# Sums of blocks in place of block products in the second layer of a routed mixture of experts

## The chip, the cores and the metric

The kernel runs on one core of a Trainium2 chip. The core has a matrix engine (TensorE, PE in the profile), a vector engine (VectorE, DVE), a scalar engine (ScalarE, ACT), a general engine (GpSimd, POOL), a queue for transfers (SyncE, SP) and 16 DMA engines. The metric is the device time of one execution in microseconds (us), lower being better.

## The reference

The program is an RWKV-5 attention followed by a balanced mixture of experts, all in float32.

```python
for t in range(S):                        # attention: B=4, H=8, S=768, D=48
    cur = einsum('bhd,bhe->bhde', u*k[t], v[t])
    y[t] = einsum('bhd,bhde->bhe', r[t], state + cur)
    state = w*state + einsum('bhd,bhe->bhde', k[t], v[t])
x = y as 3072 tokens of 384
logits = x @ w_gate                       # 8 experts, 384 tokens each, given out greedily
for e in range(8):                        # w1[e]: 384 x 1024, w2[e]: 1024 x 384
    h = maximum(x[mask_e] @ w1[e], 0)
    out[mask_e] = h @ w2[e]
```

The change touches the last line: for each expert a product of a 384x1024 and a 1024x384 matrix.

## The kernel before, in words

The first 130 us or so are the attention (class `Mild`), in units of 128 time steps, with its order on the engines written out by hand. It leaves the tokens as rows in DRAM (`x_rows`) and the logits in `LG`.

Which tokens an expert gets is found on the chip (class `Assignment`). For each expert, `likely_steps` runs three rounds: VectorE compares the best logits with 16 thresholds (`ind`), TensorE counts (`counts`, L901), VectorE sums up (`own`, `cnt`, `wide`), TensorE spreads the sum over the partitions (L912), and VectorE narrows the thresholds (`most` to `cand`, `low`). Then come the expert's number (`fmax`), two small matmuls (`st_ps`) and the places of its tokens. `tokens` makes a list of token numbers from the places with the matmuls `some_ps` (L1365) and `list_ps` (L1383). `fetch` then gathers the token rows with GpSimd (`xg`, L1468) and loads the expert's weights over SP (L1461): w1 and then w2, 1.5 MB each. The weights and `xg` lie in two turns of buffers, so expert n's weights can be loaded when expert n-2 is done with them. Routing for expert n+1 is written ahead of expert n's layers.

The expert that gets enough tokens in the first part of the sequence is treated first with 256 tokens (`early`, lines L1539 and L1547), interleaved by hand with the routing of the next ones; its other 128 tokens come last. Between these, seven experts with all their 384 tokens are treated in `Experts.run`. For each:

- `turn` transposes the gathered rows (L1483), three blocks of 128 tokens.
- `hidden` (L1492) makes the hidden layer turned: 8 blocks j of 128 hidden numbers, each with three matmuls of 384 columns (all tokens), and a relu on ScalarE (L1494) into `hid`.
- `result` (L1504) makes the second layer for one block c of 128 tokens: 8 matmuls, over j, with `hid[:, j, block c]` as the stationary operand and `w2[:, j, :]` (384 columns) streamed. ScalarE copies the sum out (L1510) and GpSimd scatters the rows to the output (L1498). The transposes of the next expert stand ahead of the last block.

In this part a scheduler orders each engine's instructions when the program is built. It interleaves the routing with the matmuls; the order is fixed on the chip[...]. The call that names the next expert's routing is one line, at the head of each expert:

```python
ahead = next(later, None)
hid = self.hidden(w1, xT, nb * 128)
```

A second form of the whole computation stands behind a branch on `have["ok"]`, for inputs on which the quick routing doesn't hold.

Of the kernel before, what the change touches and what calls it, by code (L numbers as in the profile page):

```python
# [10 lines left out]
F32 = mybir.dt.float32  # L11
# [5 lines left out]
ALU = mybir.AluOpType  # L17
# [671 lines left out]
class Assignment:  # L689
# [716 lines left out]
def rwkv5_eagle_then_base_layer_balanced(  # L1406
# [12 lines left out]
    nc = tc.nc  # L1419
    N, DX = out.shape  # L1420
    E, _, F = moe_w1.shape
    NT = N // 128
# [13 lines left out]
    o_last = keep.tile([128, DX], F32, name="o_last")  # L1436
    tok_last = keep.tile([128, 1], I32, name="tok_last")

    class Experts:

        def __init__(self):
# [4 lines left out]

        def open_rest(self, ctx, **how):
            pool = lambda name, bufs, **kw: ctx.enter_context(tc.tile_pool(name=name, bufs=bufs, **kw))
            self.h, self.o = pool("f_h", 2, **how), pool("f_o", 3, **how)
            self.ps_t, self.ps_h, self.ps_o = (pool(f"f_ps_{x}", 2, space=PSUM) for x in "tho")  # L1450

        def load_weights(self, n, fmax):
            number = walk.outs.tile([1, 1], I32, name="number")
            nc.vector.tensor_scalar(out=number, in0=fmax[0:1, :], scalar1=1.0, scalar2=float(E),
                                    op0=ALU.max, op1=ALU.min)
            pool = self.turns[n % 2]
            w1, w2 = pool.tile([128, KD, F], F32, name="w1"), pool.tile([128, KF, DX], F32, name="w2")
            e = nc.values_load(number[0:1, 0:1], engines=(mybir.EngineType.SP,), min_val=1, max_val=E,
                               skip_runtime_bounds_check_because="held between 1 and E")
            for t, src in ((w1, moe_w1), (w2, moe_w2)):  # L1460
                nc.sync.dma_start(t, src[ds(E - e, 1)].rearrange("o (c p) f -> p (o c) f", p=128))  # L1461
            return w1, w2

# [20 lines left out]
                nc.scalar.copy(xT[:, :, ts(c, 128)], xT_ps)  # L1484
            return xT

        def hidden(self, w1, xT, m):
            hid = self.h.tile([128, KF, CAP], F32, name="hid")
            for j in range(KF):
                h_ps = self.ps_h.tile([128, CAP], F32, name="h_ps")  # L1490
                for f in range(KD):
                    nc.tensor.matmul(h_ps[:, 0:m], w1[:, f, ts(j, 128)], xT[:, f, 0:m],  # L1492
                                     start=(f == 0), stop=(f == KD - 1))
                nc.scalar.activation(hid[:, j, 0:m], h_ps[:, 0:m], AF.Relu)  # L1494
            return hid

        def scatter(self, o_sb, tok, to):
            nc.gpsimd.indirect_dma_start(out=to, out_offset=bass.IndirectOffsetOnAxis(ap=tok, axis=0),  # L1498
# [14 lines left out]
        def run(self, ahead, later, rows):  # L1513
            xT = self.turn(ahead)
            while ahead:
                _, _, tok, w1, w2 = ahead
                nb = tok.shape[1]
                ahead = next(later, None)
                hid = self.hidden(w1, xT, nb * 128)
                for c in range(nb):  # L1520
                    if c == nb - 1 and ahead:
                        xT = self.turn(ahead)
                    self.result(c, hid, w2, tok, next(rows))
# [31 lines left out]
    with ExitStack() as whole:  # L1555
        x = Experts()
        for i in range(2):
            x.open(whole, i)
        rows = iter(out_rows)
        have = {}  # L1560
        first = walk.new_outs()
        with ExitStack() as part:
            mild = Mild(tc, r, k, v, w, u, moe_w_gate, x_dram, LG, ident, walk)
            mild.open(part)
            epool = part.enter_context(tc.tile_pool(name="f_early", bufs=1))

# [12 lines left out]
            def step(n, at):  # L1579
                for _ in range(steps.count((n, at))):  # L1580
                    next(early)

            with tc.manual_schedule():
                two, one = mild.run(step)
                NE = walk.EARLY // 128
                pieces = x.early(mild.ps, epool, *have["w"], *have["x"], rows, have)

                def go(m):
                    for _ in range(m):
                        next(pieces, None)  # L1590
# [12 lines left out]
                tok = walk.tokens(first["place"])  # L1603
                walk.between = lambda: None
                xg = x.gather(1, tok)
                to = walk.in_order(tok)
                walk.leave(first)
                next(early)
                have["to"] = walk.in_order(have["x"][1])
                second = walk.new_outs()  # L1610
                search = walk.likely_steps(**second)
                go(6)
                for m in (2, 3, 2, 3):
                    next(search)
                    go(m)
                go(99)
                walk.book(first, first=True)
        x.open_rest(whole, reuse_waits="tile")

        def later():  # L1620
            for _ in search:
                pass
            walk.bound(ident)
            was = second
            walk.book(was)
            walk.leave(was)
            for n in range(2, E):
                rest = n == E - 1
                now = walk.remainder() if rest else walk.event()
                walk.book(now, surely=rest)  # L1630
                walk.choose(was, now)
                yield x.fetch(n, was["fmax"], walk.tokens(was["place"]))
                if not rest:
                    walk.leave(now)
                was = now
            tc.mark_branch_hint_location("whole")
            have["ok"] = walk.found()
            yield x.fetch(E, walk.star, walk.tokens(walk.star_place, 1))

        x.run((1, xg, to, *have["v"]), later(), (a for a in [*out_rows[2:NT - 1], None]))  # L1640

    with tc.If(have["ok"] < 1, label="whole", preferred_fallthrough_block=False):
        with ExitStack() as arm:
            attention_any(arm, tc, r, k, v, w, u, moe_w_gate, x_dram, LG, ident, walk)
        walk.restart()
        with ExitStack() as arm:
            x = Experts()
            for i in range(2):
                x.open(arm, i)
            x.open_rest(arm)  # L1650
            x.run(x.fetch(0, *walk.general_fill()),
                  (x.fetch(n, *walk.general_fill()) if n < E - 1 else x.fetch(n, *walk.last_fill())
                   for n in range(1, E)), iter([out] * (NT - 1) + [None]))
    x.scatter(o_last, tok_last, out_rows[NT - 1])


# [26 lines left out]
```

## Time and profile before

| | |
|---|---|
| median of 3 runs | 416.0 us (415.75 to 416.31) |
| the profiled execution's own time | 415.83 us |
| its span, first to last instruction | 414.1 us, mean granted TensorE clock 0.989 |
| busy: PE, weight loads (PEld), DVE, ACT, POOL | 394.4, 268.3, 200.0, 153.6, 134.6 us |
| hidden layer L1492, all records | 122.2 us |
| second layer L1504, all records | 117.6 us |
| weights of an expert | 2 transfers of 1536 KB |

A line of the timeline has the start (us from the span's start), the duration, the engine, the line of the program, the operation, the tiles written and read, shapes, and how many instructions are merged; in brackets, how long the engine was idle before it and what ended that. Float32 matmuls have two records each. A table by stretches gives each engine's busy time and the number of its instructions in each stretch of the span, the granted clock (PEclk), the share of the DMA engines and their rate.

### The profile page before, as it was taken

To read this page: it belongs to the slowest core of one execution; us is meant where nothing else is said; L and a number is where in the kernel's file an instruction comes from. 1 tells how busy PE (TensorE), PEld (TensorE's weight loads), DVE (VectorE), ACT (ScalarE), POOL (GpSimd) and SP (SyncE) were. 2 spreads that over 40 slices of the span, in tenths; PEclk is the share of its full clock that TensorE was granted. 3 is DMA by queue.
4 is the path that set the end of the run, shared out by engine and by line. 5 is a ranking of instruction groups with operands and counts; after the bars stand their busy time and mean duration, and the time that the engine had idled before them with its cause. 6 is when DMAs were issued, how large, how long until landed. Compare 5 with 4: busy or idle time off the path is not lost.

```text
span 414.1 us, 7993 instructions
## 1 busy us (share of the span) xinstructions
PE 394.4 (95%) x2981; PEld 268.3 (65%) x2981; DVE 200.0 (48%) x794; ACT 153.6 (37%) x401; POOL 134.6 (33%) x172
## 2 busy tenths in 40 slices
PE   5999999999999888999999999999999999999993
PEld 4778888888877655555556555555655655655581
DVE  5776776576885788780580381273074050010000
ACT  2597888788872312212121120221221221212120
POOL 5597878566732022004104103103002121110100
PEclk9799999999999999999999999999999999999998
DMA  9999998887591282047045137109108653350010
GB/s 123 163 154 195 197 169 153 157 169 156 123 321 41 78 298 101 2 142 258 21 180 201 38 91 291 39 10 352 38 21 311 240 173 109 138 190 5 19 39 25
DMA packets 95298, 57.25 MB, mean 138 GB/s; under 512 B 77201, under 2 KB 89490, under 8 KB 95250
## 3 DMA queue, kind: packets, MB, share of 16 engines
q1 hardware_dynamic: 91520, 47.19, 45.7%
q0 software_dynamic: 3072, 9.44, 6.4%
q8 instruction: 25, 0.41, 0.4%
q14 instruction: 23, 0.19, 0.2%
q10 hardware_dynamic: 658, 0.01, 0.1%
HBM read 47.20 MB, written 9.44 MB: 137 GB/s over the span
## 4 chain that ended last, share of the span: by engine, by line
PE 71%; DMA 12%; DVE 6%; issue 5%; ACT 2%; POOL 1%; POOLq 0%; ACTq 0%; DVEq 0%
PE h_ps L1492 21%; PE o_ps L1504 19%; DMA out_dram<-o_sb,to 11%; PE y_ps L532 7%; PE g_ps L494 5%; PE kT_ps L456 3%; PE kv_ps L511 3%; PE rT_ps L462 2%; PE x_ps L581 2%; PE e_o_ps L1547 2%; PE lg_ps L561 2%; PE xT_ps L1483 2%; ACT AT L484 1%; PE e_h_ps L1539 1%; POOL xg L1468 1%
## 5 line engine op out<-in xcount | busy, mean ns | idle before, releaser
L1492 PE MATMUL h_ps<-xT,w 128*128 128x384 f32 (+1 forms) x384 | 122.2, 469 | 0.6 <-ACT xT L1484 0.6
L1504 PE MATMUL o_ps<-w,hid 128*128 128x384 f32 x352 | 117.6, 487 | 0.0
L1504 PEld LDWEIGHTS o_ps<-w,hid 128*128 128x128 f32 x352 | 65.4, 190 | 42.4 <-issue 0.8
L1492 PEld LDWEIGHTS h_ps<-xT,w 128*128 128x128 f32 x384 | 65.6, 190 | 36.5 <-issue 3.6
L1494 ACT ACTIVATE hid<-h_ps 128x384 f32<-128x384 f32 (+1 forms) x64 | 29.7, 464 | 92.2 <-PE h_ps L1492 85.3
L484 ACT ACTIVATE AT<-ident,dd 128x128 f32<-128x128 f32 x192 | 58.7, 390 | 2.1 <-DVE dd L443 1.9
L1468 POOL DMA_INDIRECT xg<-x_rows,tok x22 | 21.3, 966 | 116.2 <-issue 58.9
L1498 POOL DMA_INDIRECT out_dram<-o_sb,to x21 | 20.8, 993 | 98.1 <-ACT o_sb L1510 66.4
L1510 ACT COPY o_sb<-o_ps 128x384 f32<-128x384 f32 x21 | 10.1, 479 | 95.5 <-PE o_ps L1504 86.8
L498 DVE COPY_PREDICATED AT<-mask,g_ps 128x512 f32<-128x512 uint8 x48 | 32.6, 734 | 12.5 <-PE g_ps L494 12.2
L889 DVE TENSOR_TENSOR own<-counts,same 128x64 f32<-128x64 f32 x21 | 4.7, 225 | 65.5 <-PE counts L901 65.5
L494 PE MATMUL g_ps<-rT,kT 48*128 48x128 f32 x384 | 28.2, 287 | 0.6 <-DVE AT L498 0.6
L431 POOL TENSOR_TENSOR kss<-krs,wk 128x384 f32<-128x384 f32 x24 | 24.3, 1015 | 10.7 <-DVE krs L340 9.0
L494 PEld LDWEIGHTS g_ps<-rT,kT 48*128 48x128 f32 x384 | 23.6, 189 | 3.8 <-PE rT_ps L462 0.8
L532 PE MATMUL y_ps<-AT,vts 128*64 128x128 f32 x384 | 25.7, 276 | 0.0
L438 POOL TENSOR_TENSOR rk<-rk,u_bc 128x384 f32<-128x384 f32 x24 | 24.2, 1008 | 3.7 <-ACT u_bc L407 1.9
L437 POOL TENSOR_TENSOR rk<-krs 128x384 f32<-128x384 f32 x24 | 24.5, 1019 | 0.0
L532 PEld LDWEIGHTS y_ps<-AT,vts 128*64 128x64 f32 x384 | 20.6, 137 | 1.0 <-issue 0.5
L550 ACT COPY x<-y_ps 128x512 f32<-128x512 f32 x24 | 14.0, 585 | 15.9 <-PE y_ps L532 15.9
L474 DVE TENSOR_TENSOR rT<-rT_ps,WR 112x512 f32<-112x512 f32 x23 | 15.8, 685 | 4.4 <-PE rT_ps L462 4.3
L462 PE MATMUL rT_ps<-ident,krs 128*112 128x128 f32 x96 | 15.3, 285 | 0.0
L581 PE MATMUL x_ps<-ident,x 112*128 112x112 f32 x96 | 13.3, 262 | 1.4 <-ACT xr L588 0.7
(270 smaller groups left out, 464.6 us busy)
## 6 DMA issues: line engine op xcount, KB each, us to landing
w<-in_moe_w_dram SPq DMA_DIRECT2D x18, 1536.0 KB, 8.3
krs<-in_k_dram SPq DMA_DIRECT2D x24, 192.0 KB, 4.1
krs<-in_r_dram SPq DMA_DIRECT2D x24, 192.0 KB, 4.7
vts<-in_v_dram SPq DMA_DIRECT2D x24, 192.0 KB, 4.5
x_rows<-xr SPq DMA_DIRECT2D x24, 192.0 KB, 2.9
xg<-x_rows,tok POOLq DMA_INDIRECT x22, 4.7
out_dram<-o_sb,to POOLq DMA_INDIRECT x21, 2.6
wp<-in_w_dram SPq DMA_DIRECT2D x2, 0.4 KB, 2.0
```

The lines of the kernel that those rows point to most:

```text
L431: self.nc.gpsimd.tensor_mul(self.kss[:, n % self.NS].rearrange("p (g h) d -> p g h d", g=2)[:, :, :, 0:D], src, self.wk.rearrange("p (g h) ...
L437: nc.gpsimd.tensor_mul(rk, self.krs[:, n % self.NK, 1, 0:H, 0:D], self.krs[:, n % self.NK, 0, 0:H, 0:D])
L438: nc.gpsimd.tensor_mul(rk, rk, self.u_bc)
L462: nc.tensor.transpose(rT_ps[0:P, a, :], self.pair(kr[:, 1], a), self.ident)
L484: nc.scalar.mul(AT[:, z, a, :], self.ident, dd[:, h:h + 1])
L494: nc.tensor.matmul(g_ps[:, z, a, :], kT[rows, a, :], rT[rows, a, :], start=True, stop=True)
L498: nc.vector.copy_predicated(out=AT[:, z], mask=self.mask.unsqueeze(1).to_broadcast([128, HP, T]), data=g_ps[:, z])
L532: nc.tensor.matmul(yv[q * PD:(q + 1) * PD, o // 2, o % 2, :], lhsT, rhs, start=(o // 2, q) not in seen, stop=stop, skip_group_check=True)
L1468: nc.gpsimd.indirect_dma_start(out=xg[:, c, :], out_offset=None, in_=x_dram[0:within, :], in_offset=bass.IndirectOffsetOnAxis(ap=tok[:, c: ...
L1492: nc.tensor.matmul(h_ps[:, 0:m], w1[:, f, ts(j, 128)], xT[:, f, 0:m], start=(f == 0), stop=(f == KD - 1))
L1494: nc.scalar.activation(hid[:, j, 0:m], h_ps[:, 0:m], AF.Relu)
L1504: nc.tensor.matmul(o_ps, hid[:, j, ts(c, 128)], w2[:, j, :], start=(j == 0), stop=(j == KF - 1))
```

## The change

The second layer of the seven full experts is computed with fewer, smaller products and with sums of blocks.

In five experts (the first five in order) the first two blocks of tokens, the two halves of the hidden numbers and the two halves of the output columns form a product of two 2x2 matrices of blocks. It is made by seven products instead of eight. `S1` to `S4` are sums of hidden blocks, `T1` to `T4` sums of w2 blocks, and the outputs are sums of the products p1 to p7. Each product is four matmuls of 192 columns. The third block of tokens stays with `result`.

In the last two full experts (`many`) all three blocks, two halves and three column blocks of 128 form a 3x2 by 2x3 product, made by fifteen products instead of eighteen, each four matmuls of 128 columns. There are 10 sums of w2 blocks (`W...`), 11 of hidden blocks (`H...`) and 20 for the outputs.

All sums are instructions on VectorE. ScalarE copies the products out of PSUM in groups. Buffers for sums exist once each (`f_sums`, bufs=1), so a sum for the next expert is written when the product that reads the old one is done. w2 is loaded ahead of w1. Routing for the next expert is no longer all at the head of an expert: `later` yields between its steps, and `at_product` takes two steps during the products, so that the first count for the expert after the next stands in the second layer.

```diff
-            self.h, self.o = pool("f_h", 2, **how), pool("f_o", 3, **how)
+            self.h, self.o, self.sums = pool("f_h", 2, **how), pool("f_o", 2, **how), pool("f_sums", 1, **how)
...
-            for t, src in ((w1, moe_w1), (w2, moe_w2)):
+            for t, src in ((w2, moe_w2), (w1, moe_w1)):
...
                 nc.scalar.activation(hid[:, j, 0:m], h_ps[:, 0:m], AF.Relu)
+                if j == KF // 2 - 1:
+                    half(hid)
...
+        SEVEN_EARLY = (("S3", "h0", SUB, "h2"),)
+        SEVEN_LATE = (("S1", "h2", ADD, "h3"), ("S2", "S1", SUB, "h0"), ("S4", "h1", SUB, "S2"))
+        SEVEN = ((("p1", "h0", "w0"), ("p2", "h1", "w2")), (("p7", "S3", "T3"), ("p5", "S1", "T1")),
+                 (("p6", "S2", "T2"), ("p3", "S4", "w3")), (("p4", "h3", "T4"),))
...
+        EARLY_SUMS = (("H1", "h0", ADD, "h2"), ("H11", "h0", SUB, "h4"))
+        HID_SUMS = (("H8", "h1", ADD, "h3"), ("H7", "h1", SUB, "h0"), ("H9", "h1", SUB, "H11"),
+                    ("H3", "h5", SUB, "H9"), ("H0", "h1", ADD, "h2"), ("H6", "h3", ADD, "h5"),
+                    ("H5", "H11", ADD, "H6"), ("H2", "h2", SUB, "H6"), ("H12", "H2", ADD, "h4"))
...
+        PRODUCTS = ((("p4", "h4", "w1"), ("p1", "H1", "w2"), ("p11", "H11", "W11"), ("p10", "h5", "w4")),
+                    (("p8", "H8", "w5"), ("p13", "h1", "W13"), ("p7", "H7", "W7"), ("p9", "H9", "W9")),
+                    (("p3", "H3", "w3"), ("p0", "H0", "W0"), ("p14", "h2", "W14"), ("p5", "H5", "W5")),
+                    (("p12", "H12", "W12"), ("p6", "H6", "W6"), ("p2", "H2", "W2")))
...
+        def seven_w2(self, w2):
+            H, D = KF // 2, DX // 2
+            at = {f"w{2 * j + k}": w2[:, ts(j, H), ts(k, D)] for j in range(2) for k in range(2)}
+            self.sums_of(at, (("T3", "w3", SUB, "w1"), ("T1", "w1", SUB, "w0"), ("T2", "w3", SUB, "T1"),
+                              ("T4", "T2", SUB, "w2")), D)
+            return at
+
+        def sums_of(self, at, which, n=128):
+            for name, a, op, b in which:
+                kind = f"sum_{name[0] in 'TW'}_{sum(k[0] in 'TWSH' for k in at)}"
+                t = self.sums.tile([128, KF // 2, n], F32, name=name, tag=kind)
+                nc.vector.tensor_tensor(out=t, in0=at[a], in1=at[b], op=op)
+                at[name] = t
...
+        def products(self, products, out_sums, left, right, tok, rows, at_product, nk, ni):
...
+            for group, after in zip(products, out_sums):
+                m = len(group)
+                ps = self.ps_o.tile([128, m, D], F32, name="p_ps", tag="o_ps")
+                for q, (name, a, b) in enumerate(group):
+                    for j in range(KF // 2):
+                        nc.tensor.matmul(ps[:, q, :], left[a][:, j, :], right[b][:, j, :],
+                                         start=(j == 0), stop=(j == KF // 2 - 1))
+                    at[name] = res[:, n + q, :]
+                    at_product((n + q + 1) / count)
+                nc.scalar.copy(res[:, n:n + m, :], ps)
+                n += m
+                for name, a, op, b in after:
+                    if name not in at:
+                        at[name] = res[:, count + sum(k[0] not in "po" for k in at), :]
+                    nc.vector.tensor_tensor(out=at[name], in0=at[a], in1=at[b], op=op)
+            for c in range(ni):
+                self.leave(o_sb[:, c, :], tok[:, c:c + 1], next(rows))
...
         def run(self, ahead, later, rows):
...
-                ahead = next(later, None)
-                hid = self.hidden(w1, xT, nb * 128)
-                for c in range(nb):
+                whole = nb == NC
+                many = whole and n in (E - 2, E - 1)
+                ahead = next((a for a in later if a), None)
+                right = (self.fifteen_w2 if many else self.seven_w2)(w2) if whole else None
...
+                def at_product(part):
+                    nonlocal xT, stage
+                    if stage == 0 and part > 0.55 or stage == 1 and part > 0.75:
+                        next(later, None)
+                        stage += 1
+                        if many and stage == 2 and ahead:
+                            xT = self.turn(ahead)
...
+                hid = self.hidden(w1, xT, nb * 128, half if whole else lambda hid: None)
+                if whole:
+                    self.sums_of(left, self.HID_SUMS if many else self.SEVEN_LATE)
+                    (self.fifteen if many else self.seven)(left, right, tok, rows, at_product)
+                    if many:
+                        continue
+                for c in range(NC - 1 if whole else 0, nb):
                     if c == nb - 1 and ahead:
                         xT = self.turn(ahead)
                     self.result(c, hid, w2, tok, next(rows))
...
             for n in range(2, E):
                 rest = n == E - 1
-                now = walk.remainder() if rest else walk.event()
+                yield
+                if rest:
+                    yield
+                    now = walk.remainder()
+                else:
+                    now = walk.new_outs()
+                    yield from walk.likely_steps(**now)
```

More of the change, by code (lines that the diff above doesn't have):

```diff
@@ L1437, in rwkv5_eagle_then_base_layer_balanced @@
     tok_last = keep.tile([128, 1], I32, name="tok_last")
+    ADD, SUB = ALU.add, ALU.subtract
     class Experts:
@@ L1485, in turn, with hidden @@
             return xT
-        def hidden(self, w1, xT, m):
+        def hidden(self, w1, xT, m, half=lambda hid: None):
             hid = self.h.tile([128, KF, CAP], F32, name="hid")
@@ L1494, in hidden @@
                 nc.scalar.activation(hid[:, j, 0:m], h_ps[:, 0:m], AF.Relu)
-            return hid
+                if j == KF // 2 - 1:
+                    half(hid)
+            return hid
+        BLOCKS =        BLOCKS = dict(h0=(0, 0), h1=(0, 1), h2=(1, 0), h3=(1, 1), h4=(2, 0), h5=(2, 1))
+        SEVEN_EARLY = (("S3", "h0", SUB, "h2"),)
+        SEVEN_LATE = (("S1", "h2", ADD, "h3"), ("S2", "S1", SUB, "h0"), ("S4", "h1", SUB, "S2"))
+        SEVEN = ((("p1", "h0", "w0"), ("p2", "h1", "w2")), (("p7", "S3", "T3"), ("p5", "S1", "T1")),
+                 (("p6", "S2", "T2"), ("p3", "S4", "w3")), (("p4", "h3", "T4"),))
@@ new lines, in rwkv5_eagle_then_base_layer_balanced @@
+        SEVEN_OUT = ((("o0", "p1", ADD, "p2"),), (), (("u2", "p1", ADD, "p6"), ("u3", "u2", ADD, "p7"),
+                     ("u4", "u2", ADD, "p5"), ("o1", "u4", ADD, "p3"), ("o3", "u3", ADD, "p5")),
+                     (("o2", "u3", SUB, "p4"),))
+        EARLY_SUMS = (("H1", "h0", ADD, "h2"), ("H11", "h0", SUB, "h4"))
+        HID_SUMS = (("H8", "h1", ADD, "h3"), ("H7", "h1", SUB, "h0"), ("H9", "h1", SUB, "H11"),
+                    ("H3", "h5", SUB, "H9"), ("H0", "h1", ADD, "h2"), ("H6", "h3", ADD, "h5"),
+                    ("H5", "H11", ADD, "H6"), ("H2", "h2", SUB, "H6"), ("H12", "H2", ADD, "h4"))
@@ new lines, in rwkv5_eagle_then_base_layer_balanced @@
+        W2_SUMS = (("W11", "w0", "w3"), ("W7", "w0", "w1"), ("W9", "W7", "w3"), ("W13", "W9", "w4"),
+                   ("W0", "W13", "w5"), ("W14", "W0", "w2"), ("W12", "w0", "w2"), ("W5", "W12", "w3"),
+                   ("W6", "W5", "w5"), ("W2", "W6", "w4"))
+        PRODUCTS = ((("p4", "h4", "w1"), ("p1", "H1", "w2"), ("p11", "H11", "W11"), ("p10", "h5", "w4")),
[3 rows of a table added]
+        OUT_SUMS = ((),
+                    (("x", "p9", SUB, "p4"), ("u", "x", SUB, "p7"), ("o0", "u", ADD, "p11"), ("t", "p13", SUB, "p11"),
+                     ("o1", "t", SUB, "x"), ("o7", "p10", ADD, "p4")),
+                    (("o6", "u", ADD, "p3"), ("y", "p13", ADD, "p14"), ("z", "y", SUB, "p0"), ("o2", "p1", SUB, "z"),
+                     ("o5", "z", ADD, "p8"), ("d", "p11", SUB, "p5"), ("v", "p1", ADD, "d")),
+                    (("g", "p12", SUB, "o6"), ("o3", "g", SUB, "v"), ("q", "p6", SUB, "o5"), ("o8", "q", ADD, "v"),
+                     ("a", "p14", SUB, "p2"), ("b", "p10", ADD, "p6"), ("o4", "a", SUB, "b")))
@@ new lines, in fifteen_w2 @@
+        def fifteen_w2(self, w2):
+            H = KF // 2
+            at = {f"w{j * KD + k}": w2[:, ts(j, H), ts(k, 128)] for j in range(2) for k in range(KD)}
+            self.sums_of(at, ((name, a, ADD, b) for name, a, b in self.W2_SUMS), 128)
+            return at
[4 more added lines that the diff above has]
+                              ("T4", "T2", SUB, "w2")), D)
+            return at
@@ new lines, in sums_of, with fifteen @@
+        def sums_of(self, at, which, n=128):
[4 more added lines that the diff above has]
+                at[name] = t
+        def fifteen(self, left, right, tok, rows, at_product):
+            self.products(self.PRODUCTS, self.OUT_SUMS, left, right, tok, rows, at_product, KD, NC)
@@ new lines, in seven @@
+        def seven(self, left, right, tok, rows, at_product):
+            self.products(self.SEVEN, self.SEVEN_OUT, left, right, tok, rows, at_product, 2, 2)
+        def products(self, products, out_sums, left, right, tok, rows, at_product, nk, ni):
+            D = DX // nk
+            count = sum(len(group) for group in products)
+            own = sum(name[0] not in "po" for group in out_sums for name, _, _, _ in group)
+            res = self.sums.tile([128, count + own, D], F32, name=f"res{count}")
+            o_sb = self.o.tile([128, NC, DX], F32, name="o_all")
+            at = {f"o{i * nk + k}": o_sb[:, i, ts(k, D)] for i in range(ni) for k in range(nk)}
+            n = 0
+            for group, after in zip(products, out_sums):
[15 more added lines that the diff above has]
+                self.leave(o_sb[:, c, :], tok[:, c:c + 1], next(rows))
@@ L1497, in scatter, with leave @@
+        def leave(self, o_sb, tok, to):
+            if to is None:
+                nc.scalar.copy(o_last, o_sb)
+                nc.vector.tensor_copy(tok_last, tok)
+            else:
+                self.scatter(o_sb, tok, to)
         def scatter(self, o_sb, tok, to):
@@ L1515, in run, with half @@
             while ahead:
-                _, _, tok, w1, w2 = ahead
+                n, _, tok, w1, w2 = ahead
                 nb = tok.shape[1]
-                ahead = next(later, None)
-                hid = self.hidden(w1, xT, nb * 128)
-                for c in range(nb):
+                whole = nb == NC
+                many = whole and n in (E - 2, E - 1)
+                ahead = next((a for a in later if a), None)
+                right = (self.fifteen_w2 if many else self.seven_w2)(w2) if whole else None
+                left = {}
+                def half(hid):
+                    for name, (i, j) in self.BLOCKS.items():
+                        left[name] = hid[:, ts(j, KF // 2), ts(i, 128)]
+                    self.sums_of(left, self.EARLY_SUMS if many else self.SEVEN_EARLY)
+                def at_product(part):
[5 more added lines that the diff above has]
+                            xT = self.turn(ahead)
+                stage = 0
+                hid = self.hidden(w1, xT, nb * 128, half if whole else lambda hid: None)
[5 more added lines that the diff above has]
+                for c in range(NC - 1 if whole else 0, nb):
                     if c == nb - 1 and ahead:
@@ L1620, in later @@
         def later():
-            for _ in search:
-                pass
+            yield from search
             walk.bound(ident)
@@ L1628, in later @@
                 rest = n == E - 1
-                now = walk.remainder() if rest else walk.event()
+                yield
+                if rest:
+                    yield
+                    now = walk.remainder()
+                else:
+                    now = walk.new_outs()
+                    yield from walk.likely_steps(**now)
                 walk.book(now, surely=rest)
@@ L1635, in later @@
                 was = now
+            yield
+            yield
             tc.mark_branch_hint_location("whole")
@@ L1650, in rwkv5_eagle_then_base_layer_balanced, with others @@
             x.open_rest(arm)
-            x.run(x.fetch(0, *walk.general_fill()),
-                  (x.fetch(n, *walk.general_fill()) if n < E - 1 else x.fetch(n, *walk.last_fill())
-                   for n in range(1, E)), iter([out] * (NT - 1) + [None]))
+            def others():
+                for n in range(1, E):
+                    yield
+                    yield
+                    yield x.fetch(n, *(walk.general_fill() if n < E - 1 else walk.last_fill()))
+            x.run(x.fetch(0, *walk.general_fill()), others(), iter([out] * (NT - 1) + [None]))
     x.scatter(o_last, tok_last, out_rows[NT - 1])
```

## The prediction

> **What bounds the kernel now.** I first cut the span into stretches, one expert each.
>
> ```profile
> core 0: us, PE busy (x) PEld busy (x) DVE busy (x) ACT busy (x) POOL busy (x), PEclk, DMA share, GB/s
> 150.00:164.70 14.70, 12.54 (x53) 6.98 (x52) 11.95 (x59) 2.63 (x6) 5.02 (x5) 1.00 0.57 210
> 199.20:232.60 33.40, 33.40 (x128) 19.61 (x128) 14.21 (x74) 6.57 (x14) 5.93 (x6) 1.00 0.36 130
> 366.00:396.30 30.30, 30.30 (x98) 17.95 (x97) 0.98 (x7) 5.27 (x11) 3.92 (x4) 1.00 0.24 80
> ```
>
> From 164.7 us on TensorE has no hole: an expert takes 33.4 us, all of them PE's, at clock 1.00, while DVE works 14 of 33. Just before, at 150 to 164.7, PE waits 2.2 us and DVE is the busy one (12.0 of 14.7). So fewer PE cycles in the experts are time, as long as nothing new makes PE wait; and DVE work added before 164.7 is at once on the path.
>
> What a matmul costs I read from the timeline, as start-to-start times, since the listed duration (487 ns) overlaps the next one.
>
> ```profile
> 249.22 10.57 PE L1504 MATMUL o_ps<-w,hid 128*128 128x384 f32 x32
> 396.64 5.52 PE L1492 MATMUL h_ps<-xT,w 128*128 128x128 f32 x48
> 401.99 1.46 PE L1504 MATMUL o_ps<-w,hid 128*128 128x384 f32 x4
> ```
>
> Each f32 matmul of the program is two records. The 384-column records start 322.5 ns apart. The last, small expert shows 128 columns with a new weight block each: (401.99-396.64)/48 = 111.5 ns. The early expert's 256-column records (L1539) start 216 ns apart. A line through 256 and 384 gives 0.832 ns a column plus 3; for 192 columns that is 162.7 ns, an estimate.
>
> The third view is the timeline at 153 us, where DVE's routing chain holds PE.
>
> ```profile
> 153.07 0.36 DVE L889 TENSOR_TENSOR prop<-LG,m 128x192 bf16<-128x192 f32 x1
> 153.42 0.55 DVE L889 TENSOR_TENSOR ind<-m,cand 128x384 bf16<-128x384 f32 x1
> 154.02 0.26 PE L901 MATMUL counts<-prop,ind 128*128 128x64 bf16 x3 [0.89 <-DVE ind L889]
> 154.32 0.22 DVE L889 TENSOR_TENSOR own<-counts,same 128x64 f32<-128x64 f32 x1 [0.36 <-PE counts L901]
> 154.58 0.28 DVE L908 TENSOR_REDUCE cnt<-own 128x8 f32<-128x72 f32 x1
> 154.90 0.29 DVE L889 TENSOR_TENSOR wide<-digit_of,cnt 128x128 f16<-128x128 f32 x1
> 155.49 0.22 PE L912 MATMUL counts<-wide,ones_h 128*128 128x128 f16 x1
> ```
>
> PE already waits 0.89 us for `ind` here.
>
> [...] The trace has no such SBUF sum, but `row` (128x768, L889) takes 944, and its follower starts 864 ns after it. I use 864 where nothing depends on it[...]. [...]
>
> **The change, part by part.**
>
> *Matmuls, seven products (five experts).* Out go 16 matmuls of 384 columns, 32 x 322.5 = 10.32 us; in come 28 of 192, 56 x 162.7 = 9.11. Saved 1.21, times 5: 6.04 us. *Fifteen (two experts).* Out 48 x 322.5 = 15.48; in 120 x 111.5 = 13.38. Saved 2.10, times 2: 4.20. Together 10.2 us.
>
> *Sums on VectorE.* Seven: 4 of 768 elements, 4 of 512, 7 of 192: 3.5 + 2.4 + 1.8 = 7.7 us an expert; with routing 22 of 32 us, so DVE has room. Fifteen: 21 x 0.6 + 20 x 0.2 = 16.6 us, in experts where DVE did 6.4 and 1.0 us. They cost nothing where PE finds each in time. Seven: after the last hidden matmul, relu ends about 0.75 us later, S1, S2, S4 are there at 1.4, 2.1, 2.8; PE needs them at 3.9, 5.2, 6.5, because p1, p2 and p7 (1.3 us each) stand ahead. Fifteen: H8 is there at 1.4 (needed at 3.6), H9 at 2.6 (6.2), H3 at 3.7 (7.1), H5 at 5.5 (9.8), H12 at 6.9 (10.7). Without that cover each late sum would stop PE by its lateness.
>
> *Weights in other order.* w2 is issued ahead of w1. Each transfer takes about 5 us, one after the other: issued at 210.88 and 211.6, they landed at 217.4 and 221.5. So w2 is there 6.2 us after issue, w1 10.6. Issue was 11.6 us into an expert's hidden layer; two hidden matmuls stand before the deciding count no longer, so 10.3 now. w1 lands at 21 us and is needed at 32: free. For the last two fetches w2 waits for the expert two back to end, w1 behind it on SP; they still land some 15 us early.
>
> *Where the sums stand.* In the changed program's order on DVE, the first expert's four T sums lie inside the routing chain shown above: T3 between `m` and `prop`, T1 after `ind`, T2 between `own` and `cnt`, T4 between `cnt` and `wide`. w2 of that expert, now first, is issued at 145.8 and there at 152. Then `prop` starts at 153.93, `ind` ends at 154.83, the counts run at 154.89 instead of 154.02: 0.87 lost. T1 ends at 155.7, T2 runs from 155.75, `cnt` at 156.6, T4 at 156.75, `wide` from 157.6 to 157.9: L912 at 158.0 instead of 155.49. PE has only four 384-column records meanwhile. `most` then starts at 158.6 instead of 155.90. From there the old chain runs on: 2.7 us lost. If DVE were half as fast at f32 sums it would be 6; if T1 to T4 were covered, 0.
>
> *First full expert's tokens.* There S1 and S2 stand between `hi`, `oh` and `vals`, and one more hidden matmul stands ahead of the place sums (0.65 us). `tok` moves 1.06 us later, with it the gathers on POOL, while PE reaches the transposes 0.9 us earlier than before. Those were just in time:
>
> ```profile
> 187.25 0.99 POOL L1468 DMA_INDIRECT xg<-x_rows,tok  x1 [23.55 <-PE o_ps L1504]
> 192.59 0.31 PEld L1483 LDWEIGHTS xT_ps<-ident,xg 128*128 128x128 f32 x3 [0.61 <-DMA xg<-x_rows,tok]
> ```
>
> With weights still on the rings until about 192, the first gather lands near 192.4 and the second near 193.0 (in unshifted times), PE is there at 191.7: about 0.9 us lost (0 to 3). In later experts `tok` is ready at the hidden layer's end, 9 us ahead.
>
> *Into the first fifteen-product expert.* Two of its W sums stand ahead of S1 of the expert before, waiting for w2. It lands at 16.5 us, when that hidden layer ends at 16.6; S1 is ready 1.9 us after that, needed at 3.9. Two us of slack, no cost.
>
> *The rest.* Four result copies on ACT (0.48 us) for three, scatters later by some us; each has a product group (2.6 us or more) or the next expert to hide in. The tail (small expert, last scatter) is as before.
>
> Sum: -10.2 + 2.7 + 0.9 = -6.6. The profiled execution took 415.83 (span 414.1 and 1.7 around it), so 409.2; the median shown is 0.2 above it: **409.4 us**.
>
> **Rivals.** (a) The early T sums cost nothing, DVE having slack I don't see: 416.0 - 10.2 = 405.8. Against it: the 0.89 us that PE waits there now. (b) The clock falls. At the start of the span PE idles 2.1 us at 5.9 and the granted clock is 0.5 from 9.1 to 15.9 us. The two new holes of 1.8 and 1.6 us lie 1.5 us apart; the same fall would cost 6.8/2 = 3.4: 412.8. Against it: a hole of 0.9 leaves the clock at 1.00. (c) w2 of the sixth expert is over 2 us late, or another sum is: each us is one us; for 2 to 3 us, 412. (d) Slower: weight loads are not hidden under shorter matmuls. The new records are 56 x 5 = 280 of 192 columns and 120 x 2 = 240 of 128, 520 together. The 6.6 us is gone when each takes 12.7 ns more (175 and 124 ns). If the listed 190 ns were the pace, seven would cost 0.32 more an expert and fifteen 7.3 more: +1.6 + 14.6 + 3.6 = 435.8. Against it: 48 records at 111.5 ns, also with a new block each.
>
> **Chances.** Forecast 0.57 (408.2 to 410.6), (a) 0.14, (b) 0.10, (c) 0.09, (d) 0.07, gains and losses in balance 0.03. Range 405.5 to 413.0: from (a) past (b) and (c), only (d) and a balance outside. This kernel can tell a change from none at about 0.2%. Faster: 0.57 + 0.14 + 0.10 + 0.09, less 0.02 for a (c) that goes on in every expert: 0.88; same 0.03 + 0.01 = 0.04; slower 0.07 + 0.01 = 0.08.
>
> **What would show it.** p_ps records 162 to 164 ns apart at 192 columns and 111 to 112 at 128; an expert with seven products at 32.2 us, one with fifteen 2.1 shorter; holes on PE of about 1.8 us ahead of the counts and 1.6 ahead of L912 near 153 to 158, laid to DVE; about 1 us at the first full expert's transposes, laid to the gather; none later, clock 1.00. The forecast is wrong if records run slower, if p5, p8 or p12 wait for DVE, or if the clock falls.

## The result and the profile after

The changed kernel takes 411.5 us (median of 4 runs, 411.3 to 411.75) where the kernel before takes 416.15 beside it: ratio 0.989, 95% interval 0.987 to 0.990, 4.65 us faster. Forecast were 6.6 us and 409.4. The profiled execution has a span of 409.8 us (before: 414.1).

The stretches of one expert each again, now cut at the changed kernel's own starts:

```profile
core 0: us, PE busy (x) PEld busy (x) DVE busy (x) ACT busy (x) POOL busy (x), PEclk, DMA share, GB/s
150.00:167.25 17.25, 12.79 (x54) 6.96 (x52) 14.96 (x62) 2.55 (x6) 5.25 (x5) 1.00 0.48 185
202.21:234.64 32.43, 32.36 (x153) 22.70 (x151) 22.49 (x89) 7.50 (x16) 6.78 (x6) 1.00 0.38 134
362.16:391.86 29.70, 29.57 (x180) 22.87 (x175) 13.46 (x42) 6.54 (x13) 3.56 (x4) 1.00 0.19 73
```

An expert with seven products takes 32.4 us (before 33.4), the last one with fifteen 29.7 (before 31.5), the clock stays at 1.00, and VectorE works 22.5 us where it worked 14.2. The first stretch, which held no product of the new kind, is 2.55 us longer, with 3.0 us more of VectorE's work in it. PE now idles 0.07 us even in the second stretch, where it had no hole.

The products' pace, from TensorE's timeline (start, us, engine, line, shapes, count; the first two lines have 192 columns, the others 128):

```profile
284.01 2.76 PE L1567 MATMUL p_ps<-w,hid 128*128 128x192 f32 x16
286.61 4.06 PE L1567 MATMUL p_ps<-T,S 128*128 128x192 f32 x24
...
378.13 1.05 PE L1567 MATMUL p_ps<-w,hid 128*128 128x128 f32 x8
379.02 1.06 PE L1567 MATMUL p_ps<-w,H 128*128 128x128 f32 x8
```

(286.61 - 284.01)/16 = 162.5 ns and (379.02 - 378.13)/8 = 111 ns: what the forecast took, weight loads and all: each load of the 128-column products is listed at 190 to 192 ns (L1567, PEld, 362 to 392 us).

Then the routing chain ahead of the first full expert, from the timelines of VectorE and TensorE:

```profile
152.87 0.95 DVE L1545 TENSOR_TENSOR T<-w 128x768 f32<-128x768 f32 x1
153.74 0.35 DVE L889 TENSOR_TENSOR prop<-LG,m 128x192 bf16<-128x192 f32 x1
154.07 0.55 DVE L889 TENSOR_TENSOR ind<-m,cand 128x384 bf16<-128x384 f32 x1
154.54 0.95 DVE L1545 TENSOR_TENSOR T<-w 128x768 f32<-128x768 f32 x1
154.68 0.26 PE L901 MATMUL counts<-prop,ind 128*128 128x64 bf16 x3 [1.62 <-DVE ind L889]
155.54 0.95 DVE L1545 TENSOR_TENSOR T<-w,T 128x768 f32<-128x768 f32 x1
156.60 0.94 DVE L1545 TENSOR_TENSOR T<-T,w 128x768 f32<-128x768 f32 x1
157.47 0.28 DVE L889 TENSOR_TENSOR wide<-digit_of,cnt 128x128 f16<-128x128 f32 x1
157.80 0.22 PE L912 MATMUL counts<-wide,ones_h 128*128 128x128 f16 x1 [1.49 <-DVE wide L889]
```

Four sums stand between `m` and `wide`. PE waits 1.62 us where it waited 0.89, and 1.49 where it didn't wait.

At the first full expert's transposes (GpSimd's first gather, then PE):

```profile
190.84 0.99 POOL L1470 DMA_INDIRECT xg<-x_rows,tok  x1 [24.59 <-PE p_ps L1567]
195.48 1.02 PE L1485 MATMUL xT_ps<-ident,xg 128*128 128x128 f32 x6 [1.17 <-DMA xg<-x_rows,tok]
```

The gather is issued 23.6 us after this expert's start (before: 22.55), and PE waits 1.17 us for it.

Where the 4.3 us of span come from, as lengths of stages (hidden layer, second layer), each from its own start:

| stage | before | after | difference |
|---|---|---|---|
| start of first full expert | 164.70 | 167.25 | +2.55 |
| first: second layer | 17.28 | 17.91 | +0.63 |
| second to fourth: hidden layers | 3 x 16.77 | 3 x 16.95 | +0.54 |
| second to fourth: second layers | 3 x 16.64 | 3 x 15.47 | -3.51 |
| fifth: both | 33.29 | 32.00 | -1.29 |
| sixth: second layer | 16.62 | 14.71 | -1.91 |
| seventh: hidden layer | 15.68 | 15.98 | +0.30 |
| seventh: second layer | 15.81 | 13.73 | -2.08 |
| small expert: hidden layer | 5.36 | 5.79 | +0.43 |

They sum to -4.34. The products are as fast as they should be. Losses stand at four kinds of places, of which the forecast had two, and the second too small.

### The profile page after: what moved, and what is told of

It is laid out like the page before. It is cut to its first block, busy times and chain, and to the rows that moved or that the text cites. A ratio compares the mean times of both kernels' runs of the same rounds, so it can differ in the third digit from the quotient of the medians.

```text
span 409.8 us, 8707 instructions
## 1 busy us (share of the span) xinstructions
PE 385.9 (94%) x3245; PEld 291.7 (71%) x3245; DVE 274.0 (67%) x951; ACT 159.3 (39%) x413; POOL 140.5 (34%) x172
## 4 chain that ended last, share of the span: by engine, by line
PE 63%; DVE 18%; DMA 11%; ACT 3%; issue 3%; POOLq 0%; ACTq 0%; DVEq 0%
PE h_ps L1494 18%; PE p_ps L1567 9%; DMA out_dram<-o_all,to 9%; PE y_ps L532 7%; PE o_ps L1594 6%; PE g_ps L494 5%; PE kv_ps L511 2%; PE kT_ps L456 2%; PE rT_ps L462 2%; PE x_ps L581 2%; PE lg_ps L561 2%; PE xT_ps L1485 2%; ACT AT L484 1%; DVE H L1545 1%; DMA xg<-x_rows,tok 1%
## 5 line engine op out<-in xcount | busy, mean ns | idle before, releaser
L1496 ACT ACTIVATE hid<-h_ps 128x384 f32<-128x384 f32 (+1 forms) x64 | 29.7, 464 | 93.7 <-PE h_ps L1494 88.4
L1470 POOL DMA_INDIRECT xg<-x_rows,tok x22 | 22.9, 1040 | 112.2 <-issue 69.6
L1588 POOL DMA_INDIRECT out_dram<-o_all,to x16 | 20.0, 1247 | 75.8 <-DVE o_all L1576 73.7
L1571 ACT COPY res<-p_ps 128x384 f32<-128x384 f32 (+2 forms) x28 | 13.2, 473 | 59.0 <-PE p_ps L1567 59.0
L1594 PE MATMUL o_ps<-w,hid 128*128 128x384 f32 x96 | 32.8, 486 | 0.0
L1594 PEld LDWEIGHTS o_ps<-w,hid 128*128 128x128 f32 x96 | 17.4, 190 | 9.8
L1567 PE MATMUL p_ps<-T,S 128*128 128x192 f32 x120 | 20.7, 327 | 0.0
L1545 DVE TENSOR_TENSOR H<-hid 128x512 f32<-128x512 f32 x12 | 7.9, 687 | 19.1 <-ACT hid L1496 19.1
L1567 PEld LDWEIGHTS p_ps<-T,S 128*128 128x128 f32 x120 | 19.6, 190 | 0.0
L1567 PEld LDWEIGHTS p_ps<-w,hid 128*128 128x128 f32 x112 | 17.3, 190 | 1.9
```

Source lines behind the costliest of these rows:

```text
L1470: nc.gpsimd.indirect_dma_start(out=xg[:, c, :], out_offset=None, in_=x_dram[0:within, :], in_offset=bass.IndirectOffsetOnAxis(ap=tok[:, c: ...
L1567: nc.tensor.matmul(ps[:, q, :], left[a][:, j, :], right[b][:, j, :], start=(j == 0), stop=(j == KF // 2 - 1))
L1594: nc.tensor.matmul(o_ps, hid[:, j, ts(c, 128)], w2[:, j, :], start=(j == 0), stop=(j == KF - 1))
```

## The experiments

My theory was that the saved TensorE time is real and is given back where sums stand ahead of routing operations in VectorE's queue, most of it at the first full expert. The rival was that each product costs something of its own, spread evenly over the seven experts. All runs were timed beside the kernel before. The start of the first full expert varies among executions that have no sums ahead of it (164.5 to 165.6 us), so parts of a us are read as stage lengths.

### The first full expert the plain way

```diff
-                whole = nb == NC
+                whole = nb == NC and n > 1
```

> The first full expert has its second layer the plain way, with no sums; everything else is the changed kernel (411.5 us). Theory 1 (the loss sits in VectorE's queue at the first full expert: holes of 1.6 and 1.5 us ahead of its place, and its tokens late): 2.55 us of holes go, and its second layer goes from 17.91 back to 17.28 us: 411.5 - 2.55 - 0.63 = 408.3 us. Theory 2 (each product costs something of its own that the listed paces hide, 5.6 us over seven experts, 0.8 each): the expert loses its 1.2 us of saved columns and gets 0.8 back: 411.9 us.

Measured: 407.97 us, ratio 0.9815 (0.9802 to 0.9828). By the ratios, six experts with products are 3.0 us faster than seven. The even overhead, which expected a loss of 0.4 us, is out. The start is at 165.1 us, and its second layer takes 16.9 us, 0.4 less than even before (more on this under the order of the transfers).

### The first expert's T sums on GpSimd

```diff
-                nc.vector.tensor_tensor(out=t, in0=at[a], in1=at[b], op=op)
+                (on or nc.vector).tensor_tensor(out=t, in0=at[a], in1=at[b], op=op)
```

with `on` being `nc.gpsimd` for the T sums of the first full expert alone.

> The four T sums of the first full expert alone are on GpSimd, about 2 us each (twice the 1.0 us that a GpSimd f32 operation of 384 elements takes in this trace), needed 25 us later; S sums and products as in the changed kernel. Theory 1 (they hold the routing operations queued behind them): the two holes ahead of the counts go, the first full expert starts 2.5 us earlier, 409.0 us; its wait for tokens at the transposes stays. Theory 2 (overhead of each product): no change, 411.5. Theory 3 (GpSimd's sums slow VectorE's operations beside them): VectorE's routing operations get longer, the start is earlier by less than 1 us, 410.5 to 412.

Measured: 417.0 us, ratio 1.0031 (1.002 to 1.0042), slower than the kernel before. None of the three numbers was near; theory 3 has the mechanism, but it expected a small gain and not a loss of 5.5 us. VectorE and GpSimd in this run, from their timelines:

```profile
154.02 4.25 DVE L889 TENSOR_TENSOR prop<-LG,m 128x192 bf16<-128x192 f32 x1
154.49 3.56 POOL L1545 TENSOR_TENSOR T<-w 128x768 f32<-128x768 f32 x2
158.12 1.81 POOL L1545 TENSOR_TENSOR T<-w,T 128x768 f32<-128x768 f32 x1
158.19 1.75 DVE L987 SCALAR_TENSOR_TENSOR low<-cell,value 128x1 f32<-128x1 f32 x1
159.87 0.55 DVE L889 TENSOR_TENSOR ind<-m,cand 128x384 bf16<-128x384 f32 x1
160.01 2.07 POOL L1545 TENSOR_TENSOR T<-T,w 128x768 f32<-128x768 f32 x1
160.85 0.23 DVE L889 TENSOR_TENSOR own<-counts,same 128x64 f32<-128x64 f32 x1 [0.44 <-PE counts L901]
161.11 0.28 DVE L908 TENSOR_REDUCE cnt<-own 128x8 f32<-128x72 f32 x1
161.43 0.80 DVE L889 TENSOR_TENSOR wide<-digit_of,cnt 128x128 f16<-128x128 f32 x1
```

`prop`, 0.35 us elsewhere, takes 4.25 and ends 0.2 us after GpSimd's second sum; `low`, of one element a partition and 0.15 us in the changed kernel, takes 1.75 and ends with the third. `ind`, which starts 0.14 us ahead of the fourth sum, keeps its 0.55 us, and that sum takes 2.07 where the others take 1.80. Beside the fourth sum `own` and `cnt` keep their 0.23 and 0.28 us, and `wide`, 0.29 elsewhere, takes 0.80. `prop` and `low` are both stretched twelvefold. So a sum moved to GpSimd stays in VectorE's way here, at 1.8 us in place of 0.87: the first full expert starts at 172.7, 5.5 us later than with the sums on VectorE. What decides which operation is held, the run doesn't show: `prop` was and its record starts 0.47 us ahead of the first sum, `ind` wasn't and starts 0.14 us ahead of the fourth.

### The order of the weight transfers alone

```diff
-            for t, src in ((w1, moe_w1), (w2, moe_w2)):
+            for t, src in ((w2, moe_w2), (w1, moe_w1)):
```

in the kernel before.

> The kernel before with only the order of the two weight transfers exchanged (w2 ahead of w1). Prediction's step (free, w1 is there before it is needed): 416.15, within 0.4. Rival (w1 of the first full expert comes after its hidden layer could start at 164.7, or a later w1 is late): a hole ahead of a first hidden product, 1 us or more longer.

Measured: 415.6 us where the kernel before takes 415.7 beside it, ratio 0.9999 (0.999 to 1.0007). Free, as the forecast had it. In its profile the first second layer takes 16.92 us in place of 17.28, because the transposes there don't wait. The 0.4 us of the run with the first expert plain thus comes with this order, as far as one profile of each kernel can tell; the whole time doesn't show it.

### Fifteen products alone

```diff
-                whole = nb == NC
+                whole = nb == NC and n in (E - 2, E - 1)
```

> Five experts have their second layer the plain way; only the last two use fifteen products. Theory 1 (fifteen's gain of 2 x 2.10 less 0.3 at the seventh expert's token numbers and 0.4 in the small expert, no loss before): 416.15 - 4.2 + 0.7 = 412.65 us. Theory 2 (overhead of 0.8 an expert): 416.15 - 4.2 + 1.6 = 413.55 us.

Measured: 412.3 us, ratio 0.9914 (0.9901 to 0.9928). By the ratio that is 3.6 us less, with two experts' 4.2 forecast, and 412.6 on the scale of 416.15: theory 1's number; theory 2's lies outside the interval, which ends at 413.2. The small expert's hidden layer is 0.46 us longer here too. Against this ratio, the five experts with seven products of the changed kernel (0.9886) add 0.28%, 1.2 us, of their 6.04; without the first (0.9815), four add 0.99%, 4.1 of 4.84 us. Each ratio is good to about 0.15%, 0.6 us.

### The first expert's T sums left out

```diff
             for name, a, op, b in which:
+                if none and name[0] in none:
+                    at[name] = at[a]
+                    continue
```

with `none` being "T" for the first full expert.

> The changed kernel with the four T sums of the first full expert left out (its products take blocks of w2 in their place, so that expert's values are other ones); its S sums, products and result sums stay. Prediction's step (T sums inside the routing chain cost 2.5 to 2.7 us and nothing else): the holes of 1.6 and 1.5 us ahead of the counts near 154 and 158 us fall back to the 0.9 us of before, the first full expert starts at 164.7, its second layer still waits for tokens and still takes about 17.9 us; 411.5 - 2.55 = 408.95 us. Rival (the hole comes from the other order of the weight transfers or of the routing steps, not from the sums): first full expert still at 167.2, 411.5 us. Second rival (T sums also make the tokens late): second layer of the first full expert 17.2 us or less, 408.2 us.

Measured: 408.8 us, ratio 0.9823 (0.9805 to 0.984); 408.95 was expected. TensorE's timeline, to be laid beside the chain above:

```profile
153.97 0.26 PE L901 MATMUL counts<-prop,ind 128*128 128x64 bf16 x3 [0.89 <-DVE ind L889]
154.07 1.54 PE L1664 MATMUL e_o_ps<-w,e_hid 128*128 128x384 f32 x4
155.44 0.22 PE L912 MATMUL counts<-wide,ones_h 128*128 128x128 f16 x1
```

The 0.89 is back, the second hole is gone, and the expert starts at 164.65, 2.60 us earlier. Counted from the issue of this expert's own first gather, which comes ahead of the sums (149.97 us with them, 150.01 without), it starts 17.28 us later against 14.64, so the difference isn't the variation of the start among executions. Its second layer still takes 17.86 us: the T sums have no part in the late tokens.

### T and S sums left out

The same, with `none` being "TS".

> The changed kernel with the T and the S sums of the first full expert left out (its products take single blocks in their place, so that expert's values are other ones); products, result sums and everything else stay. It follows the run with only the T sums left out (408.84 us), where the first full expert's second layer took 17.86 us with waits of 1.17 and 0.41 us for tokens. Theory A (S sums queued in VectorE ahead of the place operations make the tokens 1.05 us late): the first gather is issued 22.5 us after the expert's start in place of 23.6, the waits shrink to under 0.5 us together, the second layer takes about 16.5 us, 407.5 us. Theory B (the tokens are late against products that are 1.2 us shorter, and the weights fill the rings until 27 us after the expert's start whatever VectorE does): the waits stay above 1 us, second layer 17.3 us or more, 408.3 us or more.

Measured: 408.2 us, ratio 0.9811 (0.9791 to 0.9832), but this profiled execution reached the first full expert 1.0 us later than the one before. From GpSimd's and TensorE's timelines:

```profile
187.87 0.99 POOL L1470 DMA_INDIRECT xg<-x_rows,tok  x1 [23.24 <-issue]
193.01 1.01 PE L1485 MATMUL xT_ps<-ident,xg 128*128 128x128 f32 x6 [0.33 <-DMA xg<-x_rows,tok]
```

The expert starts at 165.63, so the first gather is issued 22.2 us into it (23.6 with S sums), PE waits 0.33 in place of the 1.01 that the trace without T sums alone lists, and the second layer takes 16.72 us. That is theory A by the stage (16.5 expected); the whole kernel's median lies between A's and B's and can't tell them apart. Of the 17.86 us, 1.14 go with the S sums, but not by VectorE's queue alone: without them the built program also has one hidden matmul less ahead of the deciding count (0.65 us of the 1.36 by which the gather comes earlier). The run doesn't part the two.

### S3 behind the place values

```diff
-                    self.sums_of(left, self.EARLY_SUMS if many else self.SEVEN_EARLY)
+                    with tc.high_priority(offset=0 if many else -300):
+                        self.sums_of(left, self.EARLY_SUMS if many else self.SEVEN_EARLY)
```

together with the first full expert the plain way.

> The first full expert the plain way (407.97 us), and the S3 sum of the next experts moved on VectorE's order from ahead of the operations on places to behind the place values (vals) in the third and fourth; no work is added or left out. Theory (each hole of about 0.23 us ahead of the place sums, L1365, comes from the 0.6 us of S3 queued ahead of vals): the holes ahead of some_ps in the third and fourth hidden layers go, 16.95 to 16.77 us each, 407.6 us. Rival (the holes come from the count's place in TensorE's order, one matmul fewer ahead of it): they stay, 408.0 us.

Measured: 407.84 us, ratio 0.9795 (0.9777 to 0.9814). By the whole time it can't be told from the run without the move; the stages can. Of that run (first expert plain, S3 ahead), VectorE and TensorE in the third hidden layer:

```profile
241.13 0.67 DVE L1545 TENSOR_TENSOR S<-hid 128x512 f32<-128x512 f32 x1
244.99 0.44 DVE L889 TENSOR_TENSOR vals<-oh,number 128x288 f16<-128x288 f16 x1
245.47 0.31 PE L1365 MATMUL some_ps<-vals,row 128*128 128x48 f16 x6
```

and with S3 moved:

```profile
244.71 0.44 DVE L889 TENSOR_TENSOR vals<-oh,number 128x288 f16<-128x288 f16 x1
245.30 0.31 PE L1365 MATMUL some_ps<-vals,row 128*128 128x48 f16 x6
246.53 0.68 DVE L1545 TENSOR_TENSOR S<-hid 128x512 f32<-128x512 f32 x1
```

Without the move PE starts the place sums (`some_ps`) 0.04 us after `vals` ends, and the start-to-start time before them is 0.23 us too long; with it 0.15 us lies between and the hole is gone. The third hidden layer falls from 16.95 to 16.72 us, the fourth from 16.94 to 16.71 (16.77 before). The rival, TensorE's order, is out: TensorE's order in this layer is the same in both runs.

### The seventh expert

Two things left out there: the W sums, by the same edit as above, and the scatters:

```diff
             for c in range(ni):
-                self.leave(o_sb[:, c, :], tok[:, c:c + 1], next(rows))
+                to = next(rows)
+                if not (ni == NC and ahead_is_last[0]):
+                    self.leave(o_sb[:, c, :], tok[:, c:c + 1], to)
```

> The changed kernel with two things left out in the last full expert: its W sums (its products take blocks of w2 in their place) and the scatters of its three blocks (those rows of the output are not written). Theory: the hole of 0.33 us ahead of list_ps in the last full expert's hidden layer goes, as VectorE gets to the place numbers sooner (15.98 to 15.68 us); the three late records in the small expert's hidden layer (0.43 us in all) come from the scatters and go (5.79 to 5.36 us). Rivals: the list_ps hole comes from the result sums of the expert before and stays; the late records come from the longer instruction stream and stay. By the span: 409.8 - 0.7 = 409.1 us if both go.

Measured: 410.8 us (a single time), with a span of 409.1. The span meets the number by luck: of the two effects one failed and one held, and what follows the small expert's hidden layer is another 0.39 us shorter, which was not forecast. The hole ahead of `list_ps` stays without W sums (hidden layer 16.00 us). VectorE there:

```profile
364.07 0.17 DVE L889 TENSOR_TENSOR some<-some_ps,quarter 128x16 f32<-128x16 f32 x1
364.18 0.29 DVE L1580 TENSOR_TENSOR o_all<-res 128x128 f32<-128x128 f32 x1
364.39 0.17 DVE L1374 TENSOR_REDUCE part<-some 128x4 f16<-128x16 f32 x1
364.62 0.18 PE L1383 MATMUL list_ps<-part,alike 128*128 128x4 f16 x1 [0.15 <-DVE part L1374]
```

It is a result sum of the sixth expert that stands between `some` and `part`, and `some` itself starts 1.9 us after its matmuls do (364.07 against 362.14), behind six other result sums. The small expert on TensorE, first in the changed kernel and then here:

```profile
391.86 5.96 PE L1494 MATMUL h_ps<-xT,w 128*128 128x128 f32 x48
397.65 1.13 PE L1594 MATMUL o_ps<-w,hid 128*128 128x384 f32 x3
...
392.01 5.52 PE L1495 MATMUL h_ps<-xT,w 128*128 128x128 f32 x48
397.37 0.81 PE L1600 MATMUL o_ps<-w,hid 128*128 128x384 f32 x2
```

The late records went: the hidden layer is back at 5.36 us from 5.79. The W sums were left out in the same run, but in the changed kernel they end at 363.4, 28 us ahead of this layer, so this is put down to the scatters. How a scatter delays matmul records, the run doesn't show: the kernel before has a scatter's packets in the same hidden layer, from 399.2 us on, and no late record there.

### Fifteen products in the fifth expert, and all together

```diff
-                whole = nb == NC
+                whole = nb == NC and n > 1
-                many = whole and n in (E - 2, E - 1)
+                many = whole and n >= E - 3
```

> The first full expert the plain way (as in the run before, 407.97 us), and the fifth of the seven full experts with fifteen products in place of seven. If VectorE has room there (13.2 us of routing, about 16.6 of sums and, at its end, the W sums of the next, in 31 us): 2.10 - 1.21 = 0.9 us faster, 407.1 us. Rival (VectorE becomes the bound in the fourth and fifth: W and H sums stand ahead of routing operations or products wait for sums): 1 to 3 us of new holes on TensorE, 408 to 410 us.

Measured: 407.94 us, ratio 0.9798 (0.9782 to 0.9815). The fifth second layer falls by 0.69 us (15.30 to 14.61) and the sixth hidden layer grows by 0.12, where `vals` is now late (0.18 us). No product waits. Half a us by the stages, nothing that the median shows.

The last kernel has this, the S3 edit, and the small expert's token numbers put ahead:

```diff
-            yield x.fetch(E, walk.star, walk.tokens(walk.star_place, 1))
+            with tc.high_priority(offset=200):
+                at_star = walk.tokens(walk.star_place, 1)
+            yield x.fetch(E, walk.star, at_star)
```

> What the runs before point to, put together: the first full expert the plain way (407.97 us), S3 behind vals in the third and fourth (-0.48 by the two hidden layers), fifteen products in the fifth (-0.55 by its place in the trace, though its median was the same), and the small expert's token numbers moved ahead, from behind the sixth expert's result sums into the sixth expert's hidden layer (-0.29, the hole ahead of list_ps). If they add up: 406.65 us. Rival (they get in each other's way on VectorE, which works 27 of 31 us in the fifth): new holes there, 407.5 us or more.

Measured: 407.39 us, ratio 0.9794 (0.978 to 0.9809). From the first full expert's start to the end of the last scatter's issue it takes 235.46 us where the run with only the first expert plain took 236.61: -1.15 of the -1.32 expected. The seventh hidden layer falls to 15.48 us once its routing no longer stands behind result sums, but the sixth, which has the small expert's token numbers now, grows by 0.43, and its second layer falls by 0.15: 0.22 of the 0.29. This last kernel beats both the kernel before and the changed one: by the ratios it is 8.6 us under the kernel before, 3.8 under the changed one. Whether it beats the one-line edit (0.9815) by more than the measurement tells, the intervals leave open.

## Why the prediction was right, and by how much it missed

The direction, the main gain and the largest loss were right, but 411.5 us lies above the band given to the forecast (408.2 to 410.6), inside the stated range: 4.65 us of the 6.6 came.

*Matmuls, right.* 162.5 and 111 ns a record were taken and measured. Rivals (b), the clock falls, and (d), loads not hidden under shorter matmuls, are out: the clock is 1.00, with waits of 1.62 and 1.49 us in the first stretch, and the spacing is the forecast one, with loads listed at 190 to 192 ns.

*T sums in the routing chain, right.* 2.7 us forecast, 2.55 by the start of the first full expert, 2.60 by leaving the sums out. Rival (a), sums that cost nothing, is out. That an operation waits for the sums ahead of it in VectorE's queue the forecast took for granted; 2.55 and 2.60 show it for the T sums, the run with S3 moved for S3 (`vals` at 244.71 us in place of 244.99).

*First full expert's tokens: the mechanism right, the term too small.* Forecast 0.9. With no waits but those of before, its second layer would take 17.28 - 1.21 = 16.07 us; it took 17.91, 1.84 lost. The order of events was as the step had it. `tok` and the gathers are 1.04 us later (1.06 forecast); by the DMA records the first gather landed at 194.88, 27.6 us into the expert (27.7 forecast); PE was through with its products at 194.31, 27.1 us in (27.0 forecast). What the step left out: PE starts 0.60 us after the gather's last packet has landed (195.48; 0.58 in the run without T and S sums), the third block's transposes were late by another 0.30, and the place sums (`some_ps`) had already waited 0.23 for `vals`. These are 1.13, of which 0.16 stood in the 17.28 of before already; that leaves 0.97, about the 0.94 that the forecast lacks. I took a landing for a start, and one wait for the only one.

*Sums elsewhere, "no cost" and "none later": wrong.* It was worked out for the products, which indeed never waited for a sum in any run. Of the times of a sum that it used, the trace of before showed only `row`'s 864 ns; in the changed kernel's trace VectorE's sums start 0.87 us apart at 768 elements, 0.60 at 512 (0.72 where one reads the other), 0.26 at 192 and 0.20 at 128. In the second expert S1, S2 and S4 end 1.4, 2.1 and 2.9 us after the first product starts (forecast 1.4, 2.1, 2.8), in the sixth H8, H9, H3, H5 and H12 at 1.4, 2.6, 3.8, 5.6 and 7.0 (forecast 1.4, 2.6, 3.7, 5.5, 6.9). It was not worked out for the routing operations behind the sums. S3, priced at nothing, stands ahead of `vals` in each of the second to fourth experts: 0.18 us each, 0.54 in all; the move shows it for the third and the fourth, and the second has the same hole with `vals` ending 0.05 us ahead of it. Result sums ahead of `some` and `part` in the seventh: 0.30; that W sums aren't the cause is shown, that the result sums are is read from the trace.

*Scatters "later by some us", with the next expert to hide in: wrong by 0.43 us.* They cost that in the small expert's hidden layer; they went when the scatters (and, earlier, the W sums) were left out, with the mechanism open.

*Weights in other order, right*: free alone. *Into the first fifteen-product expert, right*: no hole there. Its figure of 6.2 us from issue to w2 doesn't come out of its own two times (217.4 - 210.88 = 6.5); nothing hangs on it, since S1 of the fifth expert ends at 318.55 and the product that reads it starts 3.9 us after the first one's 316.18, at 320.1.

Rival (c) gave the nearest number, 412, but not by its named place: w2 of the sixth expert made nothing wait, and in place of a late sum of 2 to 3 us there were four small stalls of routing operations behind sums. That its number is near is luck.

So 0.94 more at the first expert (1.84 - 0.9), 0.54, 0.30 and 0.43 are 2.2 us, against a span of 409.8 where 407.5 was forecast. The rest is 0.1: outside the first expert the products saved 0.25 us less than forecast (8.79 of 9.04), and the T sums cost 0.15 less.

## What to carry to other kernels

When work is added to an engine with room on average, price it against every instruction that stands behind it in that engine's queue, not only against its own consumers: here no product ever waited for its sums, and yet the routing operations behind them took nearly half of the gain (2.55 + 1.14 + 0.54 + 0.30 of 10.2 us, the 1.14 with what the built order adds). If the first pass through a loop has no slack, leave that pass as it was: one condition on `n` was worth 3.0 us. Moving such work to GpSimd was no way out here: beside its sums of 1.80 us VectorE's `prop` took 4.25 us in place of 0.35, and the first full expert started 5.5 us later than with the sums on VectorE.

## What the runs showed of the hardware

- A GpSimd f32 sum of 128x768 elements took 1.80 us (VectorE: 0.95, 0.87 from start to start). Beside the first two VectorE's `prop` took 4.25 us in place of 0.35 and ended 0.2 us after the second; `low` took 1.75 in place of 0.15 and ended with the third. An operation that started 0.14 us ahead of such a sum was not held (0.55 us), and the sum took 2.07.
- GpSimd's indirect transfers got longer in the changed kernel: 0.95 to 1.05 us an issue near the first full expert's end before, up to 1.55 for a gather and 1.93 for a scatter there, beside the second expert's T sums. No run isolates it, and in the run with the first expert plain one gather beside T sums took 0.96 and the next 1.54.
- From the last packet of a gather to the first transpose that waited for it: 0.60 us in the changed kernel, 0.55 without T sums, 0.58 without T and S sums, 0.63 with the T sums on GpSimd.
